# TensorE's work ordered in cycles of one narrow, one full-height and one half-height run, in an mLSTM with mixture-of-experts attention behind it

## The chip, the cores and the metric

The kernel runs on one core of a Trainium2 chip. The metric is the time of one execution on the device in microseconds (us), taken as the median of several runs. Engines are named as the profile names them: PE is TensorE, DVE VectorE, ACT ScalarE, POOL GpSimd, SP SyncE, which issues nearly all DMAs.

## What is computed

Two stages follow each other, in float32, for B = 4 batches of S = 768 steps. The first is a gated linear recurrence with 8 heads of 40 values (mLSTM); its output, 320 values a step, is the input x of the second, an attention with 4 experts of 64 values, of which each step takes the best two.

```python
for t in range(S):                                   # stage 1, per batch and head
    m_new = np.maximum(f_gate[:, :, t] + m, i_gate[:, :, t])
    f_stab = np.exp(f_gate[:, :, t] + m - m_new)
    i_stab = np.exp(i_gate[:, :, t] - m_new)
    C = f_stab * C + i_stab * einsum('bhd,bhe->bhde', vt, kt)
    n = f_stab * n + i_stab * kt
    h_tilde = einsum('bhde,bhe->bhd', C, qt)
    denom = np.maximum(np.abs(nq), 1.0)              # nq = n . q
    y[:, :, t] = o * h_tilde / denom                 # o = sigmoid(o_gate)
logits = x @ w_gate                                  # stage 2
topk = np.argpartition(-logits, 2, axis=-1)[..., :2]
for e in range(E):
    q, k, v = x @ wq[e], x @ wk[e], x @ wv[e]
    a = softmax(causal(scale * q @ k.T))
    ye = a @ v @ wo[e]
    out += mask[..., None] * w * ye                  # for the steps that chose e
```

## The kernel before

**Stage 1 in chunks.** Each batch is cut into 6 chunks of 128 steps, 24 chunks in all. `p1_load` fetches a chunk, `p1_prep` makes its decay matrix `dm` (POOL adds, ACT exponentials) and the scaled keys `ks`, `p1_intra` does the products of queries and keys (`qbd`, `kqs`), `p1_inc` the state's increments (`nat`, `ks`), which DVE adds to the state `sts` after POOL has decayed it (`cd`), `p1_state` the outputs (`nat`, `dm` and `sts`, `kqs`). DVE, POOL and ACT turn these into `xt`. `p1_out` transposes `xt` on PE (`cst,xt`) and ACT and DVE split the result into a rounded part `xh` and a rest `xl`. All products of stage 1 write 64 columns of the array at a time from up to 128 rows.

**Stage 2 in units.** A unit is half a batch, 384 steps, 8 units in all. Its *head* is `queries(p)` and `keys(p)` for the two pairs p of experts, `values(i)` for its three blocks of 128 steps, and `gate()`, the choice of experts. Its *body* is six batches (p, i), each with `scores` (products of `QH`, `QL` with `KH`, `KL`; DVE reads them from PSUM into `A` with the mask and finds the row's extreme; ACT takes the exponentials) and `flip` (transposes of `A` on PE, `cst,A`, copied to `AT` by ACT or DVE). `mix(p)` transposes the row factors `facb` and multiplies `AT` with `V`; `project(i)` multiplies with the output weights (`woh`, `wol`). The last unit takes `mix_rows(p, i)` for each batch instead.

**Three tile forms.** PE works on tiles of 128 x 64 (stage 1 and `AT,V`, called *narrow* here), of 128 x 128 (head, `project` and the transposes of `xt`, called *full-height*) and of 64 x 128 (`scores`, `flip`, factors, called *half-height*). Two narrow or two half-height matmuls stand side by side in the array. All PSUM tiles come from one ring, `one`, of 8 places.

**What sets the order.** The calls above only record operations on a `Tape`. In what sequence they are recorded is decided by `flow`: a clock `clk` in us is advanced by estimates that the generators yield, streams of head, body and tail are drawn by weights, and at intervals `narrow(n)` puts a chunk's stage 1 in between. Constants such as `TW`, `XD`, `AD`, `KD` are waits in that clock. `Tape.plan` then goes through the recorded groups with a cost for each operation and emits the instructions of all engines. PE groups keep their recorded order, except that `choose` takes a later group when the first would stall over 200 ns by the plan's own reckoning, and puts in spare matmuls on zeros (`wz`) where nothing else is ready. The other engines take what is ready, by due time (`late`). A group is a series of PE operations into one buffer in one form; where two buffers alternate, as in `scores` and `flip`, each matmul is a group of its own.

**The start.** Nine matmuls on zeros (`warm(9)`) and spare ones precede the first real work. `gates` computes the gates for steps 0 to 127, then 128 to 383, then 384 to 767 (DVE scans, differences on DVE or POOL); `gates_out` transposes them on PE (`cst,AT`) and DVE copies them to `cN`, which the exponentials of `dm` need.

Of the kernel before, what the change touches and what calls it, by code (L numbers as in the profile page):

```python
# [32 lines left out]
    ("A", 6, NW),  # L33
# [9 lines left out]
    ("V", 3, 3 * E * HD),  # L43
# [20 lines left out]
SH = 6  # L64
TW, NF, XD, YD, AD, KD = 5.0, 0.5, 3.2, 2.6, 2.2, 3.5
LAG = 2, 1
# [105 lines left out]
class Tape:  # L172


    def __init__(self, nc):
        self.nc, self.ops, self.masks = nc, [], {}
        self.groups, self.open, self.spares = [], None, []
        self.behind = None
        for name in ENGINES:
            setattr(self, name, Recorder(self, name))  # L180
# [21 lines left out]
    def add(self, eng, call, a, k):  # L202
# [38 lines left out]
        if pe:  # L241
            op.mm = self.matmul_time(op)
            key = outs[0].buf, op.mm[1]
# [37 lines left out]
    def cut(self):  # L281
        self.open = None
# [38 lines left out]
    def matmul_time(self, op):  # L321
# [3 lines left out]
        t = n * (1 if fast else 2 if op.call == "transpose" else 4) / 2.27 + 3  # L325
        if "float32r" in str(lhs.dtype):
            t = max(t, 0.875 * lhs.free_size())
        up = lambda x: 32 if x <= 32 else 64 if x <= 64 else 128
        mode = up(lhs.ap[0][1]), up(lhs.free_size())
        if mode == (64, 128):  # L330
            c0 = (lhs.offset // lhs.ap[0][0]) // 32
            return t, mode, range(c0, c0 + 2)
        c0 = (out.offset // out.ap[0][0]) // 32
        return t, mode, range(c0, c0 + mode[1] // 32)

    def plan(self):
        ops = self.ops
        t = 0.0
        for op in ops:
            if op.eng == "tensor":  # L340
                op.late = t
                x, mode, cols = op.mm
# [90 lines left out]
        def begin(group, fifo=True):  # L433

            r = 0.0
            for op in group:
# [5 lines left out]
                r = max(r, x)  # L442
            m = group[0].mm
# [40 lines left out]
        while len(order) < len(ops) + spare:  # L484
# [31 lines left out]
            if isinstance(op, list):  # L516
# [4 lines left out]
                for o in op:  # L521
                    x, m, cols = o.mm
# [3 lines left out]
                    extra = 55.0 if m != mode else 0.0  # L526
# [70 lines left out]
def mlstm_moe_kernel(ctx, tc, kq, nat, ig, fg, wqkv, wo, const, out):  # L597
# [28 lines left out]
    def one(name):  # L626
        return buf("one", [P, 512])
# [12 lines left out]
    warm(9)  # L640
# [188 lines left out]
    clk = [0.0]  # L829
    xr = dict.fromkeys([(b, j) for b in range(B) for j in range(NCH)], 1e9)  # L830
    ar, yr, kr = {}, {}, {}
# [55 lines left out]
    def p1_intra(b, j):  # L887
# [17 lines left out]
        yield 0.0  # L905

    def p1_inc(b, j):
# [6 lines left out]
        for sub in range(2 if j < NCH - 1 else 1):  # L914
            for g in range(2):
# [9 lines left out]
                yield 0.14  # L925
# [30 lines left out]
    def p1_state(b, j):  # L956
# [8 lines left out]
        for c in range(4):  # L965
            for sub in range(2):
# [7 lines left out]
                yield 0.07  # L974
# [3 lines left out]
        for g in range(2):  # L978
            for a in range(2):
                for sub in range(j == 0, 2):  # L980
# [7 lines left out]
                    yield 0.07  # L988
# [27 lines left out]
    def p1_out(b, j):  # L1016
# [3 lines left out]
        if jj == 0:  # L1020
# [9 lines left out]
        pxv = px[:, : 3 * P].rearrange("p (k t) -> p k t", k=3)  # L1030
        nc.scalar.activation(xh[:, :, cs], pxv, AF.Copy)
        nc.vector.tensor_tensor(xl[:, :, cs], pxv, xh[:, :, cs], op=ALU.subtract)
        xr[(b, j)] = clk[0] + 1.6

    atn = [0]
    qlu = [0] * 3
# [18 lines left out]
    def part2(b, hf):  # L1055
# [15 lines left out]
        def proj(mt):  # L1071
            while any(clk[0] < xr[(b, hf * 3 + n)] for n in range(3)):
                yield None
            pp = one(f"pp_{nm}_{mt}")
            for n, (w, x) in enumerate(passes(*xs[(b, hf)])):
# [7 lines left out]
                yield 0.16  # L1083
            return pp[:, :HALF]

        def values(i):
            while clk[0] < xr[(b, hf * 3 + i)]:
                yield None
            pv = one(f"pv_{nm}_{i}")
            for n, (w, x) in enumerate(passes(*xs[(b, hf)])):  # L1090
# [7 lines left out]
                yield 0.11  # L1098
# [3 lines left out]
        def gate():  # L1102
# [30 lines left out]
            yield 0.0  # L1133

        def queries(p):
            slot = (2 * u + p) % len(qlu)
            while qlu[slot]:
                yield None
            pq = yield from proj(2 * p)
            QH, QL = buf("QH", [P, HALF], F32R), buf("QL", [P, HALF], F32R)  # L1140
            qlu[slot] = 3
# [4 lines left out]
        def keys(p):  # L1146
            pk = yield from proj(2 * p + 1)
            nc.scalar.activation(KH[:, p, hs], pk, AF.Copy)
            nc.vector.tensor_tensor(KL[:, p, hs], pk, KH[:, p, hs].bitcast(F32), op=ALU.subtract)
            kr[u, p] = clk[0] + 1.32 + KD  # L1150

        def scores(p, i):
# [3 lines left out]
            while clk[0] < kr.get((u, p), 1e9):  # L1156
                yield None
            ar[u, p, i] = clk[0] + AD + 2 * N / 900
# [5 lines left out]
            for k in range(parts):  # L1164
                ks = slice(k * w, k * w + w)
                scs = [one(f"sc_{nm}_{p}_{i}_{ee}_{k}") for ee in range(2)]
                for n, (q, kk) in enumerate(((QHs[p], KH), (QHs[p], KL), (QLs[p], KH))):
                    for r, sc in zip(rows, scs):
                        nc.tensor.matmul(sc[:, :w], q[r, ts], kk[r, p, ks], start=n == 0, stop=n == 2)
                yield 3 * w / 2400  # L1170
# [15 lines left out]
            qlu[(2 * u + p) % len(qlu)] -= 1  # L1186

        def flip(p, i):

            while clk[0] < ar[u, p, i]:  # L1190
                yield None
            A = As.pop((p, i))
            nb = hf * 3 + i + 1
            if u == 7 or i == 0:
                while atn[0] + 1 + (hf and u < 7) > 4:
                    yield None
# [37 lines left out]
        def mix_rows(p, i):  # L1234
# [28 lines left out]
            if p:  # L1263
                yr[u, i] = clk[0] + 0.24 * nb + YD
# [370 lines left out]
```

## Time and profile before

| | us |
|---|---|
| median of 3 runs | 315.62 |
| lowest and highest of them | 315.42 and 317.71 |
| the profiled execution, its own time | 317.41 |
| its span in the profile | 315.6 |
| PE busy in the span | 306.1 |
| DVE, ACT, POOL busy | 228.0, 202.0, 174.2 |

The page of the profile gives for each engine the busy time in the span. A row of the timeline has the start in us, the duration of the whole group in us, the engine, the operation with the tiles that it writes and reads, the rows and columns of the array (128*64), the shape, the count, and in brackets the idle time before it with what ended it. Matmuls overlap, so a group's cost to PE is the distance from its start to the start of the next group, not its duration. A float32 matmul that is not of the rounded kind shows as two records. A row of the windows view has the stretch, its length, and for each engine the busy time with the number of instructions, then PE's granted clock and the share of the DMA engines.

### The profile page before, as it was taken

What the parts mean: (1) busy time and instruction counts of PE and PEld (TensorE: products, weight loads), DVE (VectorE), ACT (ScalarE), POOL (GpSimd) and SP (SyncE); (2) the same over time, 40 slices, a digit from 0 to 9 for tenths busy, and PEclk for the clock granted to TensorE, in tenths of its full rate; (3) what the DMA queues carried; (4) which work ended last, traced back from release to release, by engine and by line L of the source; (5) the groups of instructions that cost most, each with busy time, mean ns of one, the idle gap of its engine ahead of it and who ended that gap; (6) DMA issues with size and microseconds to landing.
All of it is one profiled execution on the core that took longest, in us unless ns stands there. A gap on an engine that the chain in (4) does not pass through costs nothing.

```text
span 315.6 us, 10180 instructions
## 1 busy us (share of the span) xinstructions
PE 306.1 (97%) x3815; PEld 257.0 (81%) x3815; DVE 228.0 (72%) x758; ACT 202.0 (64%) x623; POOL 174.2 (55%) x280
## 2 busy tenths in 40 slices
PE   8999799999999999999999999999999999999995
PEld 3787698798778797899888797898888897897884
DVE  7499449975996487756986487756985586469883
ACT  8684367963868178643886187742975378349681
POOL 3638478787675477866385478687385333023000
PEclk9999699999999999999999999999999999999998
DMA  7985738999653447746463446755460000100101
GB/s 220 312 222 150 215 105 247 224 214 201 162 168 94 125 141 183 225 128 170 147 173 110 129 122 179 207 162 172 125 181 4 21 3 2 44 21 2 66 23 42
DMA packets 43089, 42.94 MB, mean 136 GB/s; under 512 B 4064, under 2 KB 36800, under 8 KB 43040
## 3 DMA queue, kind: packets, MB, share of 16 engines
q1 hardware_dynamic: 42992, 42.20, 48.8%
q8 instruction: 30, 0.49, 0.6%
q14 instruction: 19, 0.16, 0.2%
q10 hardware_dynamic: 48, 0.10, 0.1%
HBM read 38.15 MB, written 4.13 MB: 134 GB/s over the span
## 4 chain that ended last, share of the span: by engine, by line
PE 76%; DVE 8%; DMA 6%; POOL 4%; ACT 3%; issue 2%; SPq 0%; POOLq 0%; ACTq 0%
PE one L579 76%; DMA dm<-gd 3%; DMA nat<-in_nat 2%; DVE A L579 2%; DVE sts L579 1%; ACT dm L579 1%; POOL dm L579 1%; DMA eqs<-ge 1%; DVE dm L579 1%; DVE one L579 1%; POOL yl L579 1%; DVE xt L579 1%; POOL ks L579 1%; ACT A L579 1%; POOL cd L579 0%
## 5 line engine op out<-in xcount | busy, mean ns | idle before, releaser
L579 ACT ACTIVATE A<-A,nmx 128x128 f32<-128x128 f32 (+5 forms) x96 | 64.0, 672 | 6.9 <-DVE nmx L579 6.8
L579 DVE CUSTOM_DVE_ANT_0 A<-one,maskw 128x384 f32<-128x384 f32 (+4 forms) x96 | 44.9, 495 | 0.7 <-PE one L579 0.4
L579 POOL TENSOR_TENSOR cd<-sts,dec 112x328 f32<-112x328 f32 x38 | 28.1, 738 | 27.0 <-DVE sts L579 26.6
L579 PE MATMUL one<-AT,V 128*64 128x384 f32 (+2 forms) x360 | 40.1, 367 | 0.1
L579 ACT ACTIVATE AT<-one 128x256 f32<-128x256 f32 (+3 forms) x96 | 33.8, 415 | 7.7 <-PE one L579 7.6
L579 PE MATMUL one<-cst,A 64*128 64x64 f32 x672 | 35.8, 229 | 1.1 <-DVE sts L579 0.3
L579 PE MATMUL one<-xh,WH 128*128 128x384 f32 x96 | 34.5, 359 | 0.4 <-ACT AT L579 0.3
L579 PEld LDWEIGHTS one<-cst,A 64*128 64x128 f32 x672 | 29.2, 138 | 6.9 <-issue 2.0
L579 PEld LDWEIGHTS one<-AT,V 128*64 128x64 f32 x360 | 22.6, 136 | 14.7 <-issue 11.8
L579 PE MATMUL one<-xl,WH 128*128 128x384 f32 x96 | 32.9, 343 | 0.0
L579 DVE TENSOR_TENSOR sts<-one,cd 40x164 f32<-40x164 f32 x80 | 25.9, 323 | 7.9 <-POOL cd L579 6.4
L579 POOL TENSOR_TENSOR dm<-dm,cst 128x512 f32<-128x512 f32 x20 | 25.6, 1284 | 10.0 <-DMA dm<-gd 9.8
L579 PE MATMUL one<-KH,QH 64*128 64x384 f32 (+4 forms) x128 | 27.8, 380 | 0.2
L579 POOL TENSOR_TENSOR kqs<-kqs,eqs 112x512 f32<-112x512 f32 x20 | 25.7, 1290 | 3.6 <-DMA eqs<-ge 2.1
L579 PE MATMUL one<-qbd,kqs 112*64 112x128 f32 x384 | 26.1, 278 | 0.0
L579 PE MATMUL one<-KL,QH 64*128 64x384 f32 (+4 forms) x128 | 26.1, 328 | 0.0
L579 PE MATMUL one<-KH,QL 64*128 64x384 f32 (+4 forms) x128 | 25.1, 325 | 0.0
L579 POOL TENSOR_TENSOR ks<-nat,dm 128x320 f32<-128x320 f32 x23 | 17.2, 746 | 13.5 <-ACT dm L579 6.7
L579 PEld LDWEIGHTS one<-qbd,kqs 112*64 112x64 f32 x384 | 20.6, 136 | 4.1 <-issue 1.7
L579 PE MATMUL one<-xh,WL 128*128 128x384 f32 x64 | 22.1, 346 | 0.0
L579 DVE COPY AT<-one 128x384 f32<-128x384 f32 (+3 forms) x48 | 21.5, 470 | 0.6 <-PE one L579 0.3
L579 PE MATMUL one<-WH,xh 128*128 128x260 f32 x72 | 20.8, 297 | 0.0
(136 smaller groups left out, 797.6 us busy)
## 6 DMA issues: line engine op xcount, KB each, us to landing
kqs<-in_kq SPq DMA_DIRECT2D x24, 448.0 KB, 4.9
nat<-in_nat SPq DMA_DIRECT2D x24, 320.0 KB, 4.7
dm<-gd SPq DMA_DIRECT2D x40, 128.0 KB, 3.2
qbd<-in_kq SPq DMA_DIRECT2D x42, 96.0 KB, 2.9
nat<-in_nat SPq DMA_DIRECT2D x48, 82.0 KB, 4.5
eqs<-ge SPq DMA_DIRECT2D x40, 96.0 KB, 3.6
out<-ob SPq DMA_DIRECT2D x24, 160.0 KB, 3.2
A<-in_wqkv SPq DMA_DIRECT2D x3, 386.0 KB, 6.3
```

The costliest lines, as they stand in the source:

```text
L579: f(*[fix(x) for x in op.a], **{k: fix(v) for k, v in op.k.items()})
```

## The change

1. `flow`, its clock, the generators' estimates and their waits are gone. The sequence is written out. For k from -1 to 6 and c from 0 to 2, a cycle records one narrow run (`p1_intra` and `p1_inc` of chunk n = 3k + 6 + c; in c = 0 and 1 the `mix` of a pair; `p1_state` of chunk n - 1), one full-height run (the parts of the next unit's head in `HEAD`; in c = 1 the three `project` of the unit before) and one half-height run (the transposes of `xt` of chunk n - 1, then two times `flip` of an earlier batch and `scores` of the next). `flip` follows `scores` by `LAG` = 2 batches. The factors' transposes are drawn from the `mix` generator at the end of the pair's last `flip`.
2. From chunk 3 on (`XW` = 3) the transposes of `xt` are half-height: six of 64 rows into two tiles instead of three of 128 rows into one, with two evictions of 64 steps each on ACT and on DVE instead of one each.
3. The last unit's scores, flips, factors, mixes and projections stand in a written sequence, `LAST`; there the factors are transposed apart from the product (`r`, then `m`).
4. `tape.cut(True)` makes alternating tiles one group, so that `choose` moves a whole pair or none; `begin` asks for as many free places as the group needs.
5. Ring `A` goes from 6 to 5 places, `V` from 3 to 4. The plan's cost of a change of form is 118 ns ahead of rounded operands and 55 ns else, where it was 55.
6. `warm(9)` becomes `warm(4)`, 40 small float32 matmuls on zeros in four 64 x 64 tiles, and `warm(4)`.

The diff, cut to its core:

```diff
-    ("A", 6, NW),
+    ("A", 5, NW),
-    ("V", 3, 3 * E * HD),
+    ("V", 4, 3 * E * HD),
-TW, NF, XD, YD, AD, KD = 5.0, 0.5, 3.2, 2.6, 2.2, 3.5
-LAG = 2, 1
+LAG, XW = 2, 3
+LAST = (
+    "f38 s40 f39 s41 q1 k1 f40 s42 f41 m38 v2 g f42 s43 m41 p6,0 f43 s44 r42 m42 p6,1 p6,2 "
+    "f44 s45 r43 m43 f45 s46 r44 m44 f46 s47 r45 m45 p7,1 f47 r46 m46 p7,2 r47 m47 p7,0"
+)
+HEAD = (
+    (
+        (("queries", 0),),
+        (("keys", 0), ("values", 2)),
+        (("gate",), ("queries", 1), ("keys", 1)),
+    ),
+    (
+        (("values", 0), ("values", 1)),
+        (("queries", 0), ("keys", 0)),
+        (("queries", 1), ("keys", 1), ("values", 2), ("gate",)),
+    ),
+)
-            key = outs[0].buf, op.mm[1]
+            key = None if self.paired else outs[0].buf, op.mm[1]
-    warm(9)
+    warm(4)
+    wq, wo2 = wz.bitcast(F32), one("wo2")
+    for n in (T, D1):
+        for _ in range(5):
+            for r, o in zip(rows, (wp, wo2)):
+                for z in rows:
+                    nc.tensor.matmul(o[z, :n], wq[r, 0:T], wq[r, 0:n], start=True, stop=True)
+    warm(4)
-        px = one(f"px_{nm}")
-        for i in range(3):
-            nc.tensor.transpose(px[:, i * P : (i + 1) * P], xf[:, i * P : (i + 1) * P], ident)
-            yield 0.11
...
+            px = [one(f"px_{nm}_{z}") for z in range(2)]
+            tape.cut(True)
+            for i in range(3):
+                for r, t in zip(rows, px):
+                    nc.tensor.transpose(t[:, i * T : (i + 1) * T], xf[r, i * P : (i + 1) * P], ident[r, r])
...
+        for cs, x in pxs:
+            nc.scalar.activation(xh[:, :, cs], x, AF.Copy)
+            nc.vector.tensor_tensor(xl[:, :, cs], x, xh[:, :, cs], op=ALU.subtract)
...
-    def flow(runs, streams, gap, first, last=False):
...
+    for k in range(-1, 7):
         if k >= 0:
...
+            parts[k + 1] = part2(*units[k + 1])
+        for c in range(3 if k < 6 else 2):
+            n = 3 * k + SH + c
+            begin(n)
+            if c < 2 and k > 0:
+                mix(6 * k - 4 + 3 * c)
+            end(n)
+            for f in HEAD[min(k + 1, 1)][c]:
+                parts[k + 1][f[0]](*f[1:])
+            if c == 1 and k > 0:
+                for i in range(3):
+                    project(k - 1, i)
+            x_of(n - 1)
+            if k >= 0:
+                for z in range(6 * k + 2 * c, 6 * k + 2 * c + 2):
+                    if z >= LAG:
+                        flip(z - LAG)
+                    score(z)
```

Counted over PE's whole instruction order, the matmuls fall into 150 runs of one form before (57 full-height, 48 half-height, 37 narrow, 8 of 32 rows) and into 116 after (39, 31, 37, 8, and one of the small matmuls on zeros). 63 transposes of `xt` move from the full-height to the half-height form, as 126.

Where it stands, first on PE in the middle of the kernel: a unit's projections. Numbers behind a name are the buffer. Before:

```order
L579 MATMUL one_65<-KL_98,QH_120 128x384
L579 MATMUL one_64<-woh_173,yh_116 128x320
...
L579 MATMUL one_67<-woh_173,yl_117 128x320
L579 MATMUL one_69<-KL_98,QH_120 128x384
L579 MATMUL one_65<-KH_96,QL_123 128x384
L579 MATMUL one_69<-KH_96,QL_123 128x384
L579 MATMUL one_68<-woh_173,yh_116 128x320
...
L579 MATMUL one_68<-woh_173,yl_117 128x320
L579 MATMUL one_66<-cst_144,xt_88 128x128 x3
L579 MATMUL one_70<-cst_144,A_78 128x64
```

And after, at the projections of a unit:

```order
L608 MATMUL one_69<-sts_158,kqs_149 64x2x41 x4
L608 MATMUL one_65<-xh_91,WH_171 128x384
...
L608 MATMUL one_70<-xl_93,WH_171 128x384
L608 MATMUL one_63<-woh_173,yh_116 128x320
...
L608 MATMUL one_64<-woh_173,yl_117 128x320
L608 MATMUL one_67<-cst_144,xt_86 128x64
L608 MATMUL one_68<-cst_144,xt_86 128x64
...
L608 MATMUL one_69<-cst_144,A_76 128x64
```

The projections have moved out of the middle of a score, to behind queries and keys, and the transposes of `xt` to the head of the half-height run.

Second, on DVE at the start, around the output of chunk 0; `AT_73<-AT_72,AT_73 32x384` is the scan over the gates of steps 384 to 767 (the profile calls it TENSOR_TENSOR_SCAN). Before:

```order
L579 RECIPROCAL den_89<-den_89 128x8
L579 TENSOR_TENSOR sts_161<-one_66,cd_86 40x4x41
L579 TENSOR_TENSOR xt_87<-one_65,den_89 128x320
...
L579 TENSOR_TENSOR xt_88<-one_70,den_90 128x320
L579 TENSOR_TENSOR one_65<-one_65,facb_136 128x328
L579 SCALAR_TENSOR_TENSOR AT_73<-AT_72,AT_73 32x384
```

After:

```order
L608 RECIPROCAL den_88<-den_88 128x8
L608 SCALAR_TENSOR_TENSOR AT_73<-AT_72,AT_73 32x384
L608 TENSOR_TENSOR xt_86<-one_66,den_88 128x320
L608 TENSOR_TENSOR sts_161<-one_67,cd_85 40x4x41 x2
...
L608 TENSOR_TENSOR sts_157<-one_69,cd_85 40x4x41
L608 COPY cN_167<-one_66 128x96
```

The scan has moved up by 14 places, and the copy of the transposed gates to `cN` stands some ten places earlier. On PE the transposes of these gates (`cst_144,AT_71`) move with it, from behind the second transposes of `xt` of chunk 2 to behind those of chunk 0. Before:

```order
L579 MATMUL one_63<-cst_144,xt_87 128x128 x3
L579 MATMUL one_67<-cst_144,AT_73 128x8
L579 MATMUL one_67<-cst_144,AT_71 64x16 x12
L579 MATMUL one_65<-AT_73,cst_144 112x24 x4
L579 MATMUL one_68<-nat_154,ks_85 40x82 x8
```

After:

```order
L608 MATMUL one_68<-cst_144,xt_86 128x128 x3
L608 MATMUL one_66<-cst_144,AT_73 128x8
L608 MATMUL one_66<-cst_144,AT_71 64x16 x12
L608 MATMUL one_67<-nat_156,dm_82 64x82 x8
```

Third, on PE in each first cycle of a unit (c = 0): the full-height run there is two `values` alone. After:

```order
L608 MATMUL one_70<-sts_162,kqs_151 64x2x41
L608 MATMUL one_63<-WH_171,xh_91 128x260
...
L608 MATMUL one_66<-WH_171,xl_93 128x260
L608 MATMUL one_68<-cst_144,xt_87 128x64
L608 MATMUL one_69<-cst_144,xt_87 128x64
```

What `sts,kqs` has finished is transposed 16 matmuls later. Before, the nearest place of that kind reads:

```order
L579 MATMUL one_65<-cst_144,A_78 128x64
L579 MATMUL one_63<-cst_144,xt_88 128x128 x3
L579 MATMUL one_64<-WH_171,xh_91 128x260
```

There the `sts,kqs` of that chunk lies a projection, a `keys` and a half-height run back.

More of the change, by code (lines that the diff above doesn't have):

```diff
@@ L442, in begin @@
                 r = max(r, x)
+                for b in op.bufs:
+                    if b.slot is None and b not in new:
+                        new[b] = b.ring
+            for ring in set(new.values()):
+                k = sum(1 for x in new.values() if x is ring)
+                if k > 1:
+                    f = sorted(ring.open())
+                    if len(f) < k + (not fifo):
+                        return None
+                    r = max(r, f[k - 1][0] + 20)
             m = group[0].mm
@@ L1380, in mlstm_moe_kernel @@
     wdum = keep("wdum", [1, 1], F32)
-    def chain(gens):
-        for g in gens:
-            yield from g
-    def drive(g):
-        for _ in g:
-            pass
     maskf = buf("R", [P, HALF], F32)
@@ L1459, in mlstm_moe_kernel @@
     parts = {0: part2(*units[0])}
-    clk[0] = 2.0
-    for n in range(2):
-        if n == 1:
-            warm(1)
-            drive(p1_out(0, 2))
-        drive(parts[0][0].pop(0))
+    parts[0]["values"](0)
+    warm(1)
+    p1_out(0, 2)
+    parts[0]["values"](1)
     gates_out(3 * P, S)
@@ L1475, in mlstm_moe_kernel, with begin, end @@
     raws.append(rawo[:, : 2 * DM])
-    asked = []
-    def narrow(n):
-        c = 0.2
-        if 0 <= n < NC:
-            drive(p1_intra(*chunks[n]))
-            drive(p1_inc(*chunks[n]))
-            c += 1.53
-        for g in asked:
-            c += sum(g)
-        asked.clear()
+    split_out_weights()
+    def begin(n):
+        if n < NC:
+            p1_intra(*chunks[n])
+            p1_inc(*chunks[n])
+    def end(n):
         if 3 <= n - 1 < NC:
-            drive(p1_state(*chunks[n - 1]))
-            c += 1.15
-        if 0 <= n and n + 2 < NC:
+            p1_state(*chunks[n - 1])
+        if n + 2 < NC:
@@ L1492, in narrow @@
             p1_load(*chunks[n + 2])
[L1493 removed]
+        if n + 1 < NC:
             p1_prep(*chunks[n + 1])
             p1_scale(*chunks[n + 1])
[L1496 to L1546 removed]
@@ L1570, in mlstm_moe_kernel, with x_of, score, flip @@
-    flow([], [(1.0, tail)], 9.0, 9.0, True)
+    def x_of(n):
+        if 3 <= n < NC:
+            p1_out(*chunks[n])
+    order = {k: [(p, i) for p in range(2) for i in range(3)] for k in range(7)}
+    order[7] = [(p, i) for i in (1, 2, 0) for p in range(2)]
+    batches = [(k, *x) for k in range(8) for x in order[k]]
+    mixing = {}
+    def score(n):
+        u, p, i = batches[n]
+        parts[u]["scores"](p, i)
+        if i == 2 and u < 7:
+            parts[u]["shares"](p)
+    def flip(n):
+        u, p, i = batches[n]
+        parts[u]["flip"](p, i)
+        if u == 7 or i == 2:
+            mixing[n] = parts[u]["mix"](*(p, i)[: 1 + (u == 7)])
+            if u < 7:
+                next(mixing[n])
@@ L1572, in mlstm_moe_kernel @@
+    h = parts[7]
+    for f in LAST.split():
+        g = dict(f=flip, r=factors, s=score, m=mix, p=project, q=h["queries"], k=h["keys"], v=h["values"], g=h["gate"])
+        g[f[0]](*[int(x) for x in f[1:].split(",") if x])
     with tc.manual_schedule(engines=set(ENGINES.values())):
```

227 lines of the change are left out of this document (53 added, 174 removed).

## The prediction

> **What bounds the kernel now.** I read the busy times of the page first, then the chain of work that ended last, then windows of single stretches (busy time and count of PE, PE's weight loads, DVE, ACT and POOL, then granted clock, DMA share, GB/s), then PE's timeline row by row.
>
> ```profile
> PE 306.1 (97%) x3815; PEld 257.0 (81%) x3815; DVE 228.0 (72%) x758; ACT 202.0 (64%) x623; POOL 174.2 (55%) x280
> PE 76%; DVE 8%; DMA 6%; POOL 4%; ACT 3%; issue 2%; SPq 0%; POOLq 0%; ACTq 0%
> ```
>
> ```profile
> 34.10:36.20 2.10, 0.03 (x2) 0.04 (x2) 0.05 (x1) 1.36 (x8) 0.82 (x2) 0.50 0.68 201
> 36.20:40.90 4.70, 4.70 (x27) 4.48 (x28) 1.94 (x5) 0.49 (x1) 2.25 (x4) 0.50 0.77 215
> 101.42:171.29 69.87, 69.78 (x895) 59.73 (x894) 50.62 (x168) 44.54 (x133) 46.39 (x71) 1.00 0.57 159
> 150.60:155.20 4.60, 4.59 (x68) 3.98 (x67) 4.60 (x18) 4.49 (x13) 1.98 (x4) 1.00 0.63 184
> ```
>
> PE carries the span: 97% busy, three quarters of the chain, and 69.78 of 69.87 us in a stretch of two units. But a busy PE is not a PE at its pace: a matmul that waits for a PSUM place, or for the array to change form, counts as busy. So the time lies in the distances between PE's starts. Two places differ from the rest: at 34.10 PE idles 2.07 us, and from there to 40.90 its clock is granted at 0.50; and between 150.60 and 155.20 DVE too is busy 4.60 of 4.60.
>
> **What a change of form costs.** PE's timeline, around a full-height run in the middle of the scores:
>
> ```profile
> 90.23 0.42 PE L579 MATMUL one<-woh,yh 128*128 128x320 f32 x1
> 90.49 0.31 PE L579 MATMUL one<-wol,yh 128*128 128x320 f32 x1
> 90.63 0.31 PE L579 MATMUL one<-woh,yl 128*128 128x320 f32 x1
> ...
> 91.07 0.31 PE L579 MATMUL one<-woh,yl 128*128 128x320 f32 x1
> 91.31 0.49 PE L579 MATMUL one<-KL,QH 64*128 64x512 f32 x1
> 91.31 0.71 PE L579 MATMUL one<-KH,QL 64*128 64x512 f32 x2
> 91.96 0.42 PE L579 MATMUL one<-woh,yh 128*128 128x320 f32 x1
> ...
> 93.05 0.96 PE L579 MATMUL one<-cst,A 64*128 64x64 f32 x24
> 93.94 0.55 PE L579 MATMUL one<-cst,xt 128*128 128x128 f32 x3
> ```
>
> Three steps from 90.63 to 91.07 are 0.147 each. The first step is 0.26 (0.11 more) and the last 0.24 (0.09 more), so a full-height run costs 0.20 beyond its matmuls. The half-height run of three scores takes 0.65; at 320 columns a step is 0.147, so at 512 it is some 0.235, and three matmuls, two side by side, are 0.35: it costs 0.30. The one of 24 transposes takes 0.89. What one costs without a change, and a transpose of `xt`, show here:
>
> ```profile
> 111.03 0.78 PE L579 MATMUL one<-cst,A 64*128 64x64 f32 x20
> 111.74 0.55 PE L579 MATMUL one<-cst,xt 128*128 128x128 f32 x3
> 112.05 0.37 PE L579 MATMUL one<-WH,xh 128*128 128x260 f32 x1
> ...
> 114.90 0.28 PE L579 MATMUL one<-WH,xl 128*128 128x260 f32 x1
> ```
>
> 20 records in 0.71 are 0.0355 each; 24 would be 0.85, so the run of 0.89 paid 0.04.
>
> **(a) Fewer changes of form, -4.3.** Full-height runs fall by 18, half-height runs by 17; I count 17 pairs. Each saves 0.20 for the full-height run and between 0.04 (half-height run of transposes) and 0.30 (of scores): -4.1 to -8.5. I take 0.05 for the half, near the low end: the half-height runs that remain mostly begin with transposes and end with scores, so the dear end of such a run stays, and what vanishes is nearer to the cheap row. -4.3.
>
> **(b) `xt` transposed half-height, -2.1.** Three of 128 rows take 0.31 (111.74 to 112.05); six of 64 at 0.0355 are 0.21. 21 chunks by 0.10 are -2.1 (with my reading error of 0.01 either way, -1.9 to -2.3). The evictions become two on ACT and two on DVE, off PE's path unless a PSUM place is missing; that is in (e).
>
> **(c) The start, -3.5.** How PE comes to idle at 34.10, in DVE, POOL, PE and ACT's rows:
>
> ```profile
> 22.20 0.20 DVE L579 RECIPROCAL den<-den 128x8 f32<-128x8 f32 x1
> 27.98 0.93 DVE L579 TENSOR_TENSOR_SCAN AT<-AT,AT 32x384 f32<-32x384 f32 x1
> 29.00 0.99 POOL L579 TENSOR_TENSOR AT<-AT,AT 32x384 f32<-32x384 f32 x1 [0.96 <-DVE AT L579]
> 31.92 1.19 PE L579 MATMUL one<-cst,AT 32*128 32x8 f32 x26
> 33.15 0.26 DVE L579 COPY cN<-one 128x96 f32<-128x96 f32 x1 [0.66 <-PE one L579]
> 33.50 1.74 ACT L579 ACTIVATE dm<-one,cN 128x64 f32<-128x64 f32 x8 [0.63 <-DVE cN L579]
> 35.38 0.73 POOL L579 TENSOR_TENSOR ks<-nat,dm 128x320 f32<-128x320 f32 x1 [2.71 <-ACT eG L579]
> 36.17 1.32 PE L579 MATMUL one<-nat,ks 128*40 128x82 f32 x16 [2.17 <-POOL ks L579]
> ```
>
> The chain is scan, differences on POOL, transposes on PE, `cN`, the exponentials of `dm`, `ks`, and PE's 2.17 us of idle in front of `nat,ks`. After the change the scan stands right behind the RECIPROCAL at 22.20, so at about 22.4: 5.6 sooner. POOL's part ends near 24.4 for 29.99, the transposes on PE can stand near 24.7 for 31.92. `cN` moves up less, since other DVE work stands in front of it, and `dm` and `ks` queue behind ACT's and POOL's work for earlier chunks; I estimate `ks` 2.2 us sooner or more, which closes the gap. What is late next is POOL, with `ks` and the decays. What the scan pushes back by 0.93 is `xt` of chunk 0 and a state's sum, whose takers on PE have the gates' work and spare matmuls ahead.
>
> The half clock costs as much again. 4.70 us of PE work ran at 0.50, which would be 2.35 at full clock; the rows show it:
>
> ```profile
> 37.90 0.52 PE L579 MATMUL one<-xh,WL 128*128 128x384 f32 x1
> 38.22 0.52 PE L579 MATMUL one<-xl,WH 128*128 128x384 f32 x1
> ...
> 41.03 0.34 PE L579 MATMUL one<-xh,WH 128*128 128x384 f32 x1
> 41.21 0.33 PE L579 MATMUL one<-xh,WL 128*128 128x384 f32 x1
> ```
>
> The same step is 0.32 at 37.90 and 0.18 at 41.03. Together the place holds 2.07 + 2.35 = 4.4. I take -3.5, since half a microsecond of idle may remain in front of `ks`; ends -4.4, and -1.0 if idle shrinks but the clock is halved all the same. In this trace the clock fell together with a pause of only 2.07 us. The Trainium skill, "TensorE: Matmul & The Clock Gate", section "Why this matters for your kernels", says to keep PE's pauses under about 3 us to avoid the drop. By that rule a shorter pause after the change keeps the full clock and (c) would be -4.4; by the row, which dropped at less, a rest of the pause could still halve it. The trace disagrees with the rule's bound here, so I do not take the whole.
>
> **(d) First work sooner, -0.5.** PE's 24 matmuls on zeros at the start, and DVE's last step of the first gates:
>
> ```profile
> 0.98 8.20 PE L579 MATMUL one<-wz 128*128 128x512 bf16 x24 [0.98 <-DVE wz L579]
> 6.55 0.59 DVE L579 TENSOR_TENSOR AT<-AT,AT 32x256 f32<-32x256 f32 x2
> ```
>
> The gates are ready at 7.14, PE goes on with zeros to 9.18: up to 2.0 are there. But the gates' next step after the first transposes hangs on loads and DVE as well, and small float32 matmuls in four tiles do not stand in this trace. In the new order 14 large ones are left ahead of the first transposes, so ten go, 3.4 at 0.34 each (8.20/24), and 40 small ones come; by the half-height transposes, 0.0355 a record, 40 of two records are 2.8. Ends -1.2 (no pace lost, first transposes near 8.0) and +0.8 (the small ones at 0.1 each); I take the difference of the two, about -0.5.
>
> **(e) Stalls, +1.3.** The new half-height runs bundle two `flip`s, two `scores` and the transposes of `xt`, all into eight PSUM places, which DVE and ACT must empty. Before has one such run, 150.60 to 155.20:
>
> ```profile
> L579 PE MATMUL one<-cst,A 64*128 64x64 f32 x36 | 2.5, 235 | 0.0
> L579 PE MATMUL one<-cst,facb 64*128 64x64 f32 x6 | 0.7, 238 | 0.0
> ```
>
> 42 transposes by 0.0355 are 1.49; the window's other 24 are scores, 12 pairs of 320 or 384 columns by 0.147 or 0.175, 1.93; with 0.2 for the form, 3.6. It took 4.60, with DVE full: a stall of 1.0. Every two units the new order has six half-height runs that write 20, 16, 16, 14, 12 and 10 tiles; the first is like that row, and and with the lighter ones at less by their tiles I estimate 2.85 us for the six, where PE's distances in before's two units, less the matmuls at the paces above, leave 2.3. Four such periods: +2.2. Then `xt`:
>
> ```profile
> 106.71 0.74 PE L579 MATMUL one<-sts,kqs 112*64 112x82 f32 x16
> 107.50 0.18 ACT L579 ACTIVATE two<-one 128x8 f32<-128x8 f32 x1 [5.48 <-PE one L579]
> 108.60 0.72 POOL L579 TENSOR_TENSOR xt<-xt,den 128x320 f32<-128x320 f32 x1 [2.33 <-PE one L579]
> 109.36 0.26 ACT L579 ACTIVATE xt<-xt 128x64 f32<-128x64 f32 x1 [0.80 <-POOL xt L579]
> ```
>
> From the end of `sts,kqs` at 107.45 to `xt` at 109.62 are 2.17. In a cycle with c = 0 only 16 `values` matmuls stand between; at (114.90 - 112.05)/23 = 0.124 that is 2.0 and 0.1 for the form. Seven such cycles wait 0.1 to 0.3: +1.4. Against this, before has waits by the same reckoning while its first units fill up, some 2.3, where the new order has lighter runs. So +2.2 + 1.4 - 2.3 = +1.3. Ends: -3 (no half-height run stalls more than now, and the cover suffices) and +8 (all six stall 1.0 or more, twice the loads of the lighter ones).
>
> The last unit's `LAST` and the rings `A` and `V` I cost at nothing: `A` holds one batch less, but `flip` follows at two batches, and the trace's end is PE work either way. If the cover fails, a `score` waits for `A`; that belongs to (e)'s upper end.
>
> **Sum.** -4.3 - 2.1 - 3.5 - 0.5 + 1.3 = -9.1. It is worked out on the profiled execution, 317.41 (span 315.6 and 1.8 around it), which lies 1.8 over the median of 315.62; the terms are differences, so I take them off the median: **306.5**.
>
> **The rivals.** *The start does not heal* (0.16): `dm` or `ks` is held by ACT, POOL or loads, PE pauses elsewhere, and the clock is halved again. For it: POOL waited 2.71 for ACT in front of `ks`, and loads take 0.68 of the DMA engines there. Against: every link of the chain moves up. Without (c) 310.0.
>
> *The half-height runs eat the gain* (0.12): each of 12 heavy runs (three in each period of two units) stalls 0.6 more than I take, +7.2: 313.7, no measurable change. For it: DVE at 4.60 of 4.60. Against: DVE has 28% free over the span, and the full-height runs between give it time.
>
> *Slower* (0.04): eviction by DVE bounds every half-height run. Before has some 12.9 us of waits in all after 43 us: 269.3 to the end of PE's work, less 237.0 of matmuls at the paces above and 19.4 of form. The time passes 318.8 when (e) reaches +13.6, so 26.5 over 31 runs, 0.85 in each. The row shows 1.0 in a heavy run, so at 1.0 in all it is 31.0 - 12.9 = +18.1: 323.3. Against: a run of 10 or 12 tiles does not fill eight places before some are empty.
>
> *The clock falls in long half-height runs* (0.02). With long stretches of transposes PE could be granted half the clock; a half-clocked window as at 34.10, 6.8 us, costs 3.4, and once in each of four periods +13.6: 320.1. In the row at 150.60, with 42 transposes of 66 matmuls, the clock is 1.00. The Trainium skill, same page, section "Part 4: PE-mode transpose", says that transposes do not count as busy for the clock. By that rule the trace should show a drop there; it does not.
>
> *Better than 302* (0.03): all pairs save 0.50 in (a) and (e) is below nothing.
>
> **How the numbers follow.** The forecast itself (302 to 309.5) gets 0.63. The range 302.0 to 312.5 takes in the first rival and holds 0.79. One per cent, 3.2 us, is about what a measurement of this kernel can tell from no change. Faster by more, under 312.5: 0.63 + 0.16 + 0.03 = 0.82; within: 0.12; slower: 0.04 + 0.02 = 0.06.
>
> **What would show it.** (a): in the windows a stretch of two units near 67.5 instead of 69.87 with (b), and full-height runs of 16 to 34 matmuls. (b): six `cst,xt` in about 0.21. (c): `cN` before 31, no pause over 0.5 us near 34, clock 1.00 to 41. (d): the first `cst,AT` before 9.1. (e): in the half-height runs, PE's starts spaced over 0.0355 and 0.175 with DVE at full; in c = 0 a gap in front of `cst,xt`. The prediction is wrong if half-height runs of 16 tiles take over 1 us more than their matmuls, or if the start's pause moves to another place.

## The result and the profile after

| | before | after |
|---|---|---|
| median, us | 315.52 (4 runs) | 305.74 (4 runs) |
| lowest and highest | 315.07, 317.71 | 304.68, 307.07 |
| ratio, 95% interval | | 0.9679 (0.962 to 0.9738) |
| profiled execution, its span | 317.41, 315.6 | 305.77, 304.0 |

The change makes the kernel 3.2% faster. Timed again beside other kernels it gave 0.9736 (0.9693 to 0.9779); a part of the difference is found below (experiments 3 and 5). The page of after, with busy time by engine, the chain that ended last, and PE's granted clock in 40 slices:

```profile
PE 292.9 (96%) x3947; PEld 251.1 (83%) x3947; DVE 226.2 (74%) x763; ACT 211.9 (70%) x665; POOL 171.7 (56%) x275
PE 63%; DVE 14%; ACT 9%; POOL 5%; DMA 3%; issue 3%; SPq 1%; DVEq 0%; POOLq 0%; ACTq 0%
PEclk9999999999999999999999999999999999999999
```

PE issues 132 more records and is busy 13 us less. DVE and ACT have risen in the chain, from 11% together to 23%: PE still sets the end, but more often by way of the engines that empty its PSUM places. In windows, two units in the middle (from the products of queries and keys of one chunk to those of the sixth after it, as the 69.87 us shown of before) and the stretch that held the pause:

```profile
82.26:150.46 68.20, 67.39 (x915) 58.82 (x913) 51.10 (x172) 46.55 (x144) 46.66 (x66) 1.00 0.63 168
34.10:40.90 6.80, 6.27 (x85) 5.40 (x83) 4.57 (x13) 5.19 (x20) 5.14 (x6) 1.00 0.90 210
```

The two units take 68.20 instead of 69.87, and between 34.10 and 40.90 PE now works 6.27 us at full clock, where it worked 4.7 us at half.

For a sum that closes I count PE's matmuls by kind, price each at its pace inside a run of one form (for most kinds before's rows in the prediction), and call *excess* what PE's starts are apart beyond that: form changes, waits, a halved clock. The level of the excess hangs on these paces, its change much less. The four lines add up to the 11.6 us by which PE's last matmul ends sooner (300.73 for 312.31):

| | before | after | change |
|---|---|---|---|
| first stage-1 matmul starts | 10.08 | 8.73 | -1.4 |
| excess from there to chunk 4 | 8.82 | 4.53 | -4.3 |
| excess from chunk 4 on | 32.33 | 29.05 | -3.3 |
| matmuls at their pace | 261.07 | 258.42 | -2.7 |

### The profile page after: what moved, and what is told of

Same layout as the page of the kernel before. It is cut to its first block, busy times and chain, and to the rows that moved or that the text cites. A ratio compares the mean times of both kernels' runs of the same rounds, so it can differ in the third digit from the quotient of the medians.

```text
span 304.0 us, 10485 instructions
## 1 busy us (share of the span) xinstructions
PE 292.9 (96%) x3947; PEld 251.1 (83%) x3947; DVE 226.2 (74%) x763; ACT 211.9 (70%) x665; POOL 171.7 (56%) x275
## 4 chain that ended last, share of the span: by engine, by line
PE 63%; DVE 14%; ACT 9%; POOL 5%; DMA 3%; issue 3%; SPq 1%; DVEq 0%; POOLq 0%; ACTq 0%
PE one L608 63%; DVE A L608 5%; DMA eqs<-ge 3%; ACT dm L608 2%; ACT A L608 2%; POOL dm L608 2%; DVE xt L608 2%; ACT AT L608 2%; DVE AT L608 1%; SPq L608 1%; DVE sts L608 1%; POOL ks L608 1%; ACT yh L608 1%; ACT V L608 1%; DVE den L608 1%
## 5 line engine op out<-in xcount | busy, mean ns | idle before, releaser
L608 ACT ACTIVATE AT<-one 128x256 f32<-128x256 f32 (+3 forms) x100 | 36.1, 428 | 4.2 <-PE one L608 3.7
L608 PE MATMUL one<-cst,A 64*128 64x64 f32 x672 | 30.6, 225 | 1.7 <-ACT A L608 1.1
L608 POOL TENSOR_TENSOR kqs<-kqs,eqs 112x512 f32<-112x512 f32 x20 | 25.7, 1283 | 10.6 <-DMA eqs<-ge 7.5
L608 PE MATMUL one<-KH,QH 64*128 64x384 f32 (+4 forms) x128 | 29.4, 380 | 1.4 <-DVE nmx L608 1.1
L608 PEld LDWEIGHTS one<-cst,A 64*128 64x128 f32 x672 | 26.4, 138 | 5.2 <-ACT A L608 2.5
L608 PE MATMUL one<-KL,QH 64*128 64x384 f32 (+4 forms) x128 | 24.6, 325 | 0.0
L608 PE MATMUL one<-KH,QL 64*128 64x384 f32 (+4 forms) x128 | 23.8, 319 | 0.0
L608 POOL TENSOR_SCALAR fac<-zs 128x6 f32<-128x6 f32 x14 | 3.4, 240 | 33.6 <-ACT A L608 33.4
L608 DVE CUSTOM_DVE_ANT_0 A<-one,maskw,nmx 128x320 f32<-128x320 f32 (+1 forms) x32 | 18.6, 582 | 3.8 <-DVE nmx L608 1.0
```

Source lines behind the costliest of these rows:

```text
L608: f(*[fix(x) for x in op.a], **{k: fix(v) for k, v in op.k.items()})
```

## The experiments

All are edits of the changed kernel, but for the first. Ratios are to the kernel before, timed beside each; the first four and the second four kernels ran on one chip, the last four on another.

**1. The kernel before, once more.** No edit.

> The kernel before, unchanged, with a second profile. If the pause at 34 us and the halved clock behind it belong to this kernel, the profile shows both again, granted clock 0.50 for some 6.8 us, and the mean clock is near 0.987 in each execution. Rival: the pause belongs to the kernel, the halved clock only to the one execution that was profiled (317.41 against a median of 315.5); then the mean clock is 1.00 in most executions, and the span of the profile is some 2 us shorter.

315.2 us, 0.9995 (0.9964 to 1.0025). Windows of its second profile:

```profile
33.00:35.16 2.16, 0.00 (x0) 0.00 (x0) 0.02 (x1) 1.45 (x9) 0.79 (x2) 1.00 0.68 195
35.16:38.60 3.44, 3.44 (x23) 3.22 (x24) 1.95 (x5) 0.00 (x0) 1.39 (x2) 0.54 0.72 202
38.60:42.00 3.40, 3.40 (x30) 3.26 (x31) 1.28 (x4) 1.53 (x5) 3.23 (x4) 0.96 0.61 176
```

The pause stands there again, 2.16 us, and the clock halves behind it, but for 3.4 us instead of 6.8. In the first profile of before, the one of the prediction, the order was another:

```profile
30.68:34.09 3.41, 3.31 (x45) 2.99 (x44) 2.47 (x7) 1.59 (x6) 1.84 (x3) 1.00 0.81 254
34.09:37.50 3.41, 1.33 (x17) 1.12 (x17) 0.69 (x1) 1.37 (x8) 1.43 (x2) 0.50 0.71 210
```

There the clock fell as the pause began, behind 3.41 us in which PE was busy for 3.31. So the first of its two halved stretches of 3.41 us can hardly come from the pause; only the second lies behind it. Nine of these ten executions have a mean clock of 0.993 to 0.994, as one halved stretch of 3.4 us makes it (1.7 of 313 us is 0.0054), and take 313.89 to 315.76 us; those of the kernel before at 0.982 and 0.983 took 318.19 and 318.62. By the mean clocks a halved stretch is in every execution of this kernel, its length differs between executions, and the profile on which I predicted had caught a long one. The excess up to chunk 4 is 8.22 here, and from there on 30.89 instead of 32.33.

**2. The scan held back.** A dependency puts the scan of steps 384 to 767 behind the sums of chunk 2.

```diff
+    late = [o for o in tape.ops if o.eng == "vector" and o.call == "tensor_tensor"][-2]
...
+        tape.behind = late if c0 == 3 * P else None
         nc.vector.tensor_tensor_scan(G_sb[:, cs], rmask[:, cs], g_sb[:, cs], 0.0, op0=ALU.mult, op1=ALU.add)
+        tape.behind = None
```

> The changed kernel, its scan over the gates of steps 384 to 767 held back until the place where it stood before. Theory (part c): the pause in front of the first scaled keys of chunk 3 comes back, 2 us, and if the clock is halved behind it 2 more: slower by 3.5 us, 2.0 to 4.4. Rival: what was gained in the start came from the other edits there; then it is slower by less than 1 us.

309.02 us, 0.9807 (0.9759 to 0.9856); against 0.9736 for the change on that chip 2.2 us slower. Its PE rows and windows:

```profile
53.84 0.58 PE L608 MATMUL one<-cst,xt 64*128 64x64 f32 x6
56.59 1.97 PE L608 MATMUL one<-qbd,kqs 112*64 112x128 f32 x16 [2.16 <-DVE xl L608]
```

```profile
54.40:56.59 2.19, 0.03 (x1) 0.00 (x1) 0.41 (x2) 2.19 (x10) 2.03 (x6) 0.67 0.73 188
56.59:61.80 5.21, 5.21 (x56) 4.97 (x57) 2.92 (x13) 0.98 (x5) 4.57 (x9) 0.50 1.08 260
```

The size is near the low end of what was expected, the place is not as expected. Up to chunk 4 its excess is 4.55, as without the edit; the pause comes 20 us later, in front of `qbd,kqs`, where ACT is busy all of 2.19 us with the exponentials of a `dm` and only then takes the transposed `xt`. The clock falls to 0.50 within the pause (at 55.16, so the window of the pause has 0.67). A late scan thus costs some 2 us here, but not by the chain that I had drawn to 34 us.

**3. Nine large matmuls on zeros.** `warm(9)` in place of `warm(4)`, the 40 small ones and `warm(4)`.

> The changed kernel with the nine large matmuls on zeros of before in place of four large, 40 small and four large. Theory (part d): the first transposes of gates start near 9.1 instead of 7.75, and the time is 0.5 to 1.4 us longer. Rival: the start is bounded by loads, DVE and POOL behind it, and the lost 1.4 us is made up by 26 us: less than 0.3.

306.62 us, 0.9711 (0.9671 to 0.975): not slower than the change on that chip (0.9736). In the profile the gates' first transposes start at 8.82 instead of 7.75, the first stage-1 matmul at 9.79 instead of 8.73, and PE ends 1.13 later, 301.86: the lost start is not made up, so the theory holds between these two executions. What makes the medians equal shows beside the change's second profile, here the windows of the change:

```profile
10.20:13.60 3.40, 3.40 (x49) 2.92 (x47) 1.83 (x4) 3.33 (x13) 2.51 (x3) 0.97 1.04 358
13.60:17.00 3.40, 3.40 (x44) 3.39 (x42) 0.87 (x3) 2.12 (x10) 1.04 (x2) 0.53 0.80 272
```

and of the kernel with nine large ones:

```profile
13.60:17.00 3.40, 3.40 (x68) 3.14 (x68) 2.12 (x6) 2.86 (x13) 1.78 (x2) 1.00 0.81 270
```

With the small ones the clock is 0.53 from 13.6 to 17.0, though PE was busy 3.40 of 3.40 us before. 44 matmuls pass instead of 68. Sorted by clock the times agree with that: in experiment 5 the change takes 305.64 us (median of three) where the mean clock is 0.997 or more and 308.62 (of three) where it is 0.994 or less; the six executions here, all at 0.999 or more, take 306.62.

**4. Projections one by one.** The three projections of a unit go between the flips and scores of the half-height run.

```diff
-            if c == 1 and k > 0:
-                for i in range(3):
-                    project(k - 1, i)
...
                         flip(z - LAG)
+                    if c == 1 and k > 0:
+                        project(k - 1, z % 2)
                     score(z)
+                    if c == 1 and k > 0 and not z % 2:
+                        project(k - 1, 2)
```

> The changed kernel with each unit's three projections put singly between the flips and scores of the half-height run instead of behind the full-height one: 150 runs of one form on TensorE instead of 116 (56 full-height, 48 half-height), as many as before the change. Theory (part a): 17 pairs by 0.25 are +4.3 us, up to +8.5. Rival: a projection between them gives DVE and ACT the time to empty PSUM places, which takes as much from the stalls (some 0.6 us in each of the six runs that are split): 0 to +1.

310.88 us, 0.9847 (0.9807 to 0.9886), 3.5 us over the change on that chip, which is less than the 4.3 forecast, but more than the rival's 1. Half of the change's executions there have a halved stretch; at full clock it is 310.75 (five executions) against 305.64 (three), 5.1 us. In the profiles PE's excess from chunk 4 on is 34.71 instead of 29.05, +5.7 for the same matmuls. The rows at one projection, in PE's timeline:

```profile
92.92 0.34 PE L608 MATMUL one<-KH,QL 64*128 64x384 f32 x2
93.19 0.41 PE L608 MATMUL one<-woh,yh 128*128 128x320 f32 x1
93.44 0.31 PE L608 MATMUL one<-wol,yh 128*128 128x320 f32 x1
...
94.03 0.31 PE L608 MATMUL one<-woh,yl 128*128 128x320 f32 x1
94.27 0.84 PE L608 MATMUL one<-cst,A 64*128 64x64 f32 x20
95.03 0.42 PE L608 MATMUL one<-woh,yh 128*128 128x320 f32 x1
```

The projection is entered 0.27 behind the last score (0.17 inside a run) and left 0.24 behind its last matmul (0.147 inside). 5.7 over 17 pairs is 0.33 each, between the 0.24 and 0.50 of the forecast. Some of it is waits and not form: where the projections no longer stand in front of a `cst,xt`, PE waits there, once for 0.62 us (at 89.86, for DVE's `xt`). The rival, that the split relieves DVE, does not show. The narrow runs have 0.9 us less of excess, but in the last unit, where a wait for ACT now falls in front of another matmul.

**5. The change once more.** No edit.

> The changed kernel as it is, timed beside the three others of this job: near 0.968 of the kernel before, clock 1.00 in each execution, since no pause of PE over 0.6 us stands in it.

306.35 us, 0.9736 (0.9693 to 0.9779), and the second half of the expectation was wrong: the mean clock was 0.992 to 0.998. It is the stretch at 13.6 to 17.0 shown above. Over all kernels with the small matmuls (but those of experiments 2 and 7, which have a halved stretch of their own) 18 of 46 executions have a mean clock under 0.996, the mark of one halved stretch; with nine large ones none of 12 (experiments 3 and 10). Five of the 18 were profiled, and in all five the stretch lies between 13.1 and 17.0 us; of the others only the mean clock is known.

**6. `xt` transposed full-height.** `XW = 24` instead of 3.

> The changed kernel with the transposes of xt full-height for all chunks, as before. Theory (part b): 21 chunks by 0.10 are +2.1 us; as the plan sets apart some of them, 8 full-height and 4 half-height runs more, +1.6 to +2.8 on top: +3.7 to +4.9. Rival: one place and two evictions for each chunk instead of two and four relieve the half-height runs by as much: within 1 us of the changed kernel.

306.93 us, 0.9752 (0.9714 to 0.979), 0.5 us over the change beside it, which the intervals do not tell from nothing: the rival. The matmuls at their pace cost 2.4 us more, as reckoned, and 12 more runs of one form come on top; yet the excess from chunk 4 on falls from the 28.50 of the change's second profile to 26.98. The half-height transposes keep a part of their gain in the middle, where two units take 68.19 us in the change and 68.77 here. They lose it while the first units fill up: between chunk 4 and chunk 9 the change has 1.9 us more of excess. One place of it, in the change (first profile) and here, PE's rows:

```profile
54.50 0.56 PE L608 MATMUL one<-cst,xt 64*128 64x64 f32 x6
55.66 1.09 PE L608 MATMUL one<-qbd,kqs 112*64 112x128 f32 x16 [0.59 <-DVE sts L608]
```

```profile
55.98 0.62 PE L608 MATMUL one<-cst,xt 128*128 128x128 f32 x3
56.52 1.09 PE L608 MATMUL one<-qbd,kqs 112*64 112x128 f32 x16
```

Behind the six half-height transposes, which take two PSUM places, PE starts `qbd,kqs` only when DVE has read a sum of the state from PSUM; behind the three full-height ones, with one place, it does not wait.

**7. `xt` transposed last.** `x_of(n - 1)` moves from the head of the half-height run to its end.

> The changed kernel with the transposes of xt at the end of each half-height run, behind the scores, instead of at its head; 116 runs as before. Theory (part e): the waits for xt in the cycles with c = 0 go, 1.3 us over seven of them, and the half-height runs of 16 and 20 tiles, where DVE is full, find two places more at their head: faster by 1.3 to 3 us. Rival: the transposes then wait behind the scores for places and xh and xl come late for the next unit's queries: the same time or slower.

305.7 us, 0.9703 (0.9676 to 0.9731), 1.0 us less than the change beside it, but the intervals overlap. Two units take 66.23 us instead of 68.19. But while unit 0 is built, its first half-height run and the narrow run behind it lose 2.8 us more than in the change, and the clock falls there: every execution has 0.981 to 0.992.

**8. Rings as before.** `A` 6 places, `V` 3.

> The changed kernel with the rings of before, six places for A and three for V. Theory: neither ring bounds anything, within 0.5 us of the changed kernel. Rival: with five places a score waits for its A in the heavy half-height runs, and six make it faster by 1 us or more; or three places for V make values wait, slower by as much.

308.65 us, 0.9789 (0.9754 to 0.9824), slower than the change beside it by 1.7 us by the ratios, whose intervals overlap a little, and 2.3 by the medians: one of the rivals. Which ring it is, experiment 11 tells.

**9. `xt` last, but not in unit 0.**

```diff
-            x_of(n - 1)
+            if k <= 0:
+                x_of(n - 1)
             if k >= 0:
...
                     score(z)
+            if k > 0:
+                x_of(n - 1)
```

> The changed kernel with the transposes of xt behind the scores of a half-height run from unit 1 on, and at its head, as in the change, only while unit 0 is built. Theory: with them behind the scores the half-height runs stall 0.3 to 0.9 less each, near 5 us over the whole, and the late xt and the halved clock that the earlier run had at 54 to 62 us do not come: 3 to 5 us faster than the changed kernel, near 0.959 of the kernel before. Rival: what was lost at 54 to 62 us belongs to the new place itself and comes back in another unit: within 1 us of the changed kernel.

302.33 us, 0.959 (0.954 to 0.9639), the fastest kernel here, and at the expected ratio. Its two units and one of its heaviest half-height runs, in windows:

```profile
81.99:148.29 66.30, 66.28 (x914) 59.12 (x912) 51.27 (x175) 44.75 (x138) 46.23 (x68) 1.00 0.64 168
101.89:106.12 4.23, 4.23 (x78) 3.91 (x77) 3.68 (x15) 3.36 (x10) 2.74 (x4) 1.00 0.93 295
```

The same run in the change:

```profile
102.16:106.94 4.78, 4.45 (x77) 3.80 (x76) 4.00 (x16) 4.39 (x13) 3.48 (x5) 1.00 0.95 287
```

4.23 us instead of 4.78, for 3.76 of matmuls; ACT's 4.39 of 4.78 shrink to 3.36 of 4.23. In the change PE stands inside this run like this:

```profile
104.57 0.66 PE L608 MATMUL one<-cst,A 64*128 64x64 f32 x16
105.04 0.41 PE L608 MATMUL one<-KH,QH 64*128 64x384 f32 x1
105.70 0.44 PE L608 MATMUL one<-KH,QH 64*128 64x384 f32 x1 [0.25 <-DVE nmx L608]
```

Half of a pair of scores has a PSUM place, the other half gets one 0.66 us later, when DVE has read a score of the batch before. With the transposes of `xt` at the head, their two places and four evictions stand ahead of the scores'; at the end they fall beside the narrow run that follows.

**10. The same with nine large matmuls on zeros.**

> The kernel before this one with the nine large matmuls on zeros at the start. Theory: the small matmuls on zeros gain 1.0 us of first work, but let the clock be halved near 13.6 to 17 us in some executions, which costs 1.6; with nine large ones the clock is 1.00 there in all executions, first work starts 1 us later, and the median is within 0.7 us of its pair. Rival: the halved stretch comes from the chip's own phase and is as frequent with nine large ones; then it is slower by 1 us.

303.21 us, 0.9609 (0.9568 to 0.965): not told apart from experiment 9. Its clocks are 0.997 to 1.00, those of experiment 9 0.991 to 0.999; there the two executions at 0.991 and 0.994 took 304.12 and 303.89, the four others 301.37 to 303.03.

**11. `V` alone with three places.**

> The changed kernel with three places for V instead of four, A at five. If V's fourth place is what the earlier run lacked, this too is 2.3 us slower than the changed kernel, most of it in the half-height runs that hold a flip while values wait and in the last unit. Rival: the loss came with the sixth place of A, by the other order in which the plan then sets scores: within 0.5 us.

309.85 us, 0.98 (0.9749 to 0.9851), as experiment 8; the excess from chunk 4 on is 31.49, 3.0 over the change's 28.50. ACT in the change's second profile, behind the `values` of a first cycle:

```profile
115.69 0.38 ACT L608 ACTIVATE V<-one 128x256 f32<-128x256 f32 x1 [0.97 <-PE one L608]
```

and with three places, PE, ACT and DVE:

```profile
118.39 0.39 PE L608 MATMUL one<-KH,QH 64*128 64x128 f32 x2 [0.27 <-DVE AT L608]
123.67 0.38 ACT L608 ACTIVATE V<-one 128x256 f32<-128x256 f32 x1 [0.72 <-PE one L608]
124.68 0.42 DVE L608 COPY V<-one 128x256 f32<-128x256 f32 x1
```

The products are ready at the same time, but wait until 123.67 and 124.68 for a place in `V`, and hold two of the eight PSUM places through the whole half-height run. The scores in it come short of places.

**12. The last unit in plain order.** Each projection stands where its mixes are done.

```diff
-    "f38 s40 f39 s41 q1 k1 f40 s42 f41 m38 v2 g f42 s43 m41 p6,0 f43 s44 r42 m42 p6,1 p6,2 "
-    "f44 s45 r43 m43 f45 s46 r44 m44 f46 s47 r45 m45 p7,1 f47 r46 m46 p7,2 r47 m47 p7,0"
+    "f38 s40 f39 s41 q1 k1 f40 s42 f41 m38 v2 g f42 s43 m41 p6,0 p6,1 p6,2 f43 s44 r42 m42 "
+    "f44 s45 r43 m43 p7,1 f45 s46 r44 m44 f46 s47 r45 m45 p7,2 f47 r46 m46 r47 m47 p7,0"
```

> The changed kernel with the last unit's sequence made plain: each projection as soon as its mixes are recorded, instead of one or two batches later. Theory (the last unit costs nothing either way): within 0.7 us of the changed kernel. Rival: the written sequence hides the chain from a mix to its projection, some 2 us, behind other work, and without it each of three projections waits: 1.5 to 4 us slower.

306.73 us, 0.9701 (0.9655 to 0.9747), not told apart from the change, as expected. Some waits come in front of the last products and the last projection but one (0.4 and 0.5 us more of excess), others go.

## Why the prediction was right, and where a step was not

The time lies within 0.8 us of the forecast, and the two largest terms, (a) and (c), are the largest. The others were off in both directions.

- **(a) Fewer changes of form**, -4.3: right. As many runs as before, put back, cost +5.7 us of excess, some of it waits; the low end had been too careful. The price of 0.2 for a full-height run shows in every row where one begins and ends. The Trainium skill, "TensorEngine Tiling (Array Packing)", section "Key Properties", says that a change of tiling mode drains the engine; these rows give its price here. Two units of the middle take 68.20 where the prediction had named 67.5 as the sign; that figure was named for (a) and (b), without the stalls of (e).
- **(c) The start**, -3.5: the size is right, the way only in part. The excess up to chunk 4 fell by 4.3, or by 3.7 against the second profile of before; the change's second profile, with its halved stretch near 14 us, has 1.3 more. The profile on which the term rests had a longer halved stretch than most executions; so the profiled executions differ by 11.6 us and the medians by 9.8. The scan, `cN` and `ks` moved up as said:

```profile
20.96 1.37 DVE L608 TENSOR_TENSOR_SCAN AT<-AT,AT 32x384 f32<-32x384 f32 x1
28.14 0.24 DVE L608 COPY cN<-one 128x96 f32<-128x96 f32 x1
31.64 0.74 POOL L608 TENSOR_TENSOR ks<-nat,dm 128x320 f32<-128x320 f32 x1 [0.93 <-ACT dm L608]
39.09 0.77 PE L608 MATMUL one<-nat,ks 128*40 128x82 f32 x16 [0.53 <-POOL ks L608]
```

  `ks` starts 3.7 us sooner, and 0.53 us of pause remains, in front of the `ks` of a later chunk. But with the scan alone held back, the pause came at 54 us and not at 34. That a scan at its old place costs 2 us is shown; that this chain alone caused the pause at 34 is not. Nor is it shown that closing the pause removed the first halved stretch, which began with the pause and not behind it (experiment 1).
- **The bet on the clock** in (c): the pause was closed, so both readings give full clock there. The prediction read the drop in before as the pause's doing, and there it was wrong for the first half of the stretch. The Trainium skill, "TensorE: Matmul & The Clock Gate", section "Why this matters for your kernels", sets a bound of about 3 us of pause. That is too wide for these runs all the same: the clock fell behind a pause of 2.18 us in the second profile of before and within one of 2.16 us in experiment 2. It also fell behind no pause at all, at 34.09 in the first profile of before and near 14 us in the change. The rival of transposes that do not count as busy work did not show: the half-height run of 4.78 us, with 52 transposes among its 77 records, has clock 1.00.
- **(b) `xt` half-height**, -2.1: failed as a gain. The matmuls saved 2.4 us, as counted, but experiment 6 gives 0.5 us in all, not told from nothing. The step that failed is that the evictions are "off PE's path unless a PSUM place is missing": the rows of experiments 6 and 9 show places missing, while the first units fill up most of all. In how many runs that is so was not counted.
- **(e) Stalls**, +1.3: too small, and not where I had looked. With form changes as many as before (experiment 4), the excess (34.71) is 2.4 over the profile on which I predicted and 3.8 over the second one. The waits for `xt` in the first cycles were sized well, some 1.3 us over the units; this is one of them, in PE's rows:

```profile
114.82 0.28 PE L608 MATMUL one<-WH,xl 128*128 128x260 f32 x1
115.39 0.56 PE L608 MATMUL one<-cst,xt 64*128 64x64 f32 x6 [0.29 <-DVE xt L608]
```

  The half-height runs of the middle were sized well too. The heavy ones take 1.0, 1.0 and 1.35 us over their matmuls, so 0.8, 0.8 and 1.15 beyond the 0.2 for the form, where I took 1.0; the six of two units stall some 2.6 us by this reckoning, where I took 2.85. What failed is the -2.3 for lighter runs while the first units fill up: between chunk 4 and chunk 9 the excess changed by -0.3 us against the first profile of before and by +0.9 against the second. The half-height runs at 53.41 and 60.80 alone take 1.5 us each over their matmuls. Of the 4.0 us of excess that experiment 9 removes (25.02 for 29.05), 3.1 lie in half-height runs and 0.9 in the full-height runs ahead of these waits.
- **(d) First work**, -0.5: the first stage-1 matmul starts 1.36 us sooner, more than I took, but only some 0.9 of that is the change. The large matmuls on zeros start 0.427 us apart at first and 0.216 later, and the moment at which this turns differs between executions: 6.78 and 4.71 us in the two profiles of before, whose first stage-1 matmul starts at 10.08 and 9.06. With the small ones and the same 6.78 us (experiment 8) it starts at 9.15. What this brings is lost again in the executions with a halved stretch near 14 us. In the medians nothing of it is left that can be told.
- **The rings**, at nothing: failed. For `A` that stands, as far as experiments 8 and 11 differ by little; the fourth place of `V` is worth 1.7 us by the ratios and 2.5 to 3.0 in the profiles. I had looked at who waits for `A` and not at what a late `V` does to the PSUM ring.

So (b) came short by 1.6 and (e) by 1.1 to 2.5, which overlap, since the evictions of (b) are among the stalls. Against them stand (a), 1.4 more than forecast, (c), up to 0.8 more, and `V`. How (a) and (e) share their sum rests on experiment 4 alone; the sum of the two, -3.0 in the forecast, is -3.3 between the first profiles. That the total comes within 0.8 us is in part luck: misses that cancel.

## What to carry to other kernels

Where matmuls of several tile forms share one array, count the runs of one form and price each by the rows at its ends; here that was the largest single term. Before a transposition or a copy is split to save time on the engine that bounds, count the buffers and evictions that the split adds, and put it where another stretch of work empties them, at the end of a burst and not at its head. A ring that looks idle can hold up another: the result that waits for a place keeps its PSUM place meanwhile. And before a gain of a microsecond at the start is believed, sort the executions by their clock: here a gain of 0.9 was hidden in the medians by a loss that more than a third of them had.

## What the runs showed of the hardware

- The granted clock was halved in stretches of 3.41 us or twice that: 34.09 to 40.91 and 35.44 to 38.85 in the two profiles of before, 55.16 to 61.98 in experiment 2, 13.41 to 16.82 in the second profile of the change. In the 3.41 us ahead of each PE was busy 3.31, 1.24, 2.29 and 3.42 us. By the mean clocks (0.994, 0.989 and 0.982) one, two or three such stretches came in executions of the same kernel.
- So a pause of 2.2 us was followed by half the clock, but a pause is not needed. The two stretches in which PE was busy nearly throughout have one thing in common: about 2 us of matmuls on 32 rows with 8 and 24 columns (31.9 to 34.0 and 10.95 to 13.0 us). That these bring the drop is not shown; the change's first profile has the same matmuls at 10.6 to 12.6 and keeps the full clock.
- When the drop near 14 us comes goes with when the clock first rose. In the ten profiles with 40 small matmuls on zeros it rose to full between 3.96 and 6.82 us. In the six where that was at 6.31 or later it was halved again 6.83 us after, in the four at 5.92 or earlier it was not halved there, nor in the four profiles with nine large ones (4.05 to 6.78 us). What ties them together was not tried.
